# Down products one step later and a weight conversion moved from step 1 to steps 2 and 3, in a retention, ELU and gated-linear kernel

## The chip, the core and the metric

The kernel runs on one core of a Trainium2 chip. The metric is the device time of one execution in microseconds (us). The core has five engines that run their own queues in order: TensorE (matmul, PE), VectorE (DVE), ScalarE (ACT), GpSimd (POOL) and SyncE (SP, which issues most DMA transfers here). An engine waits only where an instruction needs the result, or the buffer, of another.

## The reference

All data are float32. The result must be close to this:

```python
scores = q @ k.T / sqrt(D)                      # B=4, H=8, S=576, D=64
ret    = (scores * gamma_h ** (i - j) * (i >= j)) @ v
x      = ret, heads joined                      # 2304 tokens x 512
h      = x @ w_in                               # 512 x 2048
y      = where(h > 0, h, exp(min(h, 0)) - 1) @ w_out
out    = (sigmoid(y @ w_gate) * (y @ w_val)) @ w_o2   # 1536 wide
```

## The kernel before

**Numbers.** A float32 product is made of three matmuls on a rounded part ("high") and a remainder ("low") of both operands: high x high, high x low, low x high (`mm3`). So each operand is split: ScalarE copies it to the rounded type, and another engine subtracts the copy from the original to get the remainder (`split`, L109 and L110). The weights come as raw 64-bit words and are converted on the chip in a chain of five stages (`Weight.chain`): L154 and L155 on ScalarE; L157 and L158 on VectorE; L161 (VectorE); L163 (VectorE); L169 (ScalarE copy, the high part) and L172 (remainder, on GpSimd unless the caller says `dve`). A chain works in a scratch tile `t`, whose number is the third argument of `Weight`.

**Tokens and steps.** Retention runs over 18 row tiles of 128 rows (`Step`, L226). For row tile n, `block(n)` gives TensorE `inter`(n), `scores`(n+1), `outs`(n) and `sums`(n+1), all made of 64x64 matmuls; VectorE gets `causal`(n+1) (L286), `x_mul`(n) (L347), two state additions of n+1 (L308, L312) and `x_low`(n) (L361); ScalarE `x_high`(n) (L354); GpSimd the state's decay (L313) and the scaling of v of row tile n+2 (L271).

The first pass of the feed-forward is done while retention still runs. Its steps s = 0, 1, 2, ... are `ff[s]`: 256 tokens (row tiles 2j and 2j+1, j = s//2) by one block of 128 hidden columns (f = s % 2). A step has up products (12 matmuls of 256 columns, L380), the ELU (ScalarE L393 and L394, VectorE L397), its split into high (ScalarE) and remainder (L110), and down products (12 matmuls, L114 to L116). The down products of `ff[i]` need the weights `W["o", i % 2]`, which are weights[1] and weights[3], and the tile `gt` of `ff[i]`. With f = 1 they end a sum, which ScalarE copies out of PSUM (L440).

**Order.** The program order is written out by hand and is the order of every engine's queue. In step s >= 4 the block of row tile s + 2 comes first, then up products of s; in steps 2 and 3 the up products come first and then the block. In step 1 the blocks of row tiles 2 and 3 stand behind the up products, with warm-up matmuls (`warm_up`, L122, on zeros) between. Down products of s - `LAG` (`LAG` = 2) come last in a step, from step 2 on. Each call of `stage()` gives one stage of the conversion that belongs to the step (`conv`): at its start, twice within `ups`, and once within `downs` (or, with no `downs`, at the end); the fifth stage comes at the start of the next step. weights[1] is converted in step 1 by hand, all on VectorE and ScalarE; weights[3] in step 2; weights[4] to [7] in steps 6, 9, 12 and 15; the weight `W["i", 4]` begins in step 13. The ELU tile ring `g_tile` has `LAG` + 2 = 4 tiles.

**Loads.** Row tiles from 9 on are loaded in two halves; the second half waits for the end of a feed-forward product (`begin_rest`). The load of a later weight in `loads` waits for `ff[s - LAG].end`, the last product that was issued for that step.

Of the kernel before, what the change touches and what calls it, by code (L numbers as in the profile page):

```python
# [42 lines left out]
LATE = 4  # L43
SPARE = {3: 2, 8: 2, 4: 3, 9: 3, 14: 3}
LAG = 2
FIRST_APART = 9
WARM = 12, 2, 3, 5, 4, 6

# [6 lines left out]
def retention_elu_glu(  # L55
# [13 lines left out]
    pe, act, dve, pool, sp = nc.tensor, nc.scalar, nc.vector, nc.gpsimd, nc.sync  # L69
# [11 lines left out]
    class Ring:  # L81
# [5 lines left out]
        def more(self, pool, n):  # L87
            self.homes += [(pool, f"{self.name}{len(self.homes) + i}") for i in range(n)]
# [10 lines left out]
    d_tile = Ring("d", epool, 2, [128, 256], F32)  # L99
    g_tile = Ring("g", gpool, LAG + 2, [128, 2, 512], F32R)  # L100
    t_tile = Ring("t", tpool, 2, [128, DM], I32)
# [5 lines left out]
    def split(hi, lo, src, lo_engine):  # L107

        act.copy(hi, src)  # L109
        lo_engine.tensor_tensor(out=lo, in0=src, in1=hi.bitcast(F32), op=ALU.subtract)  # L110
# [7 lines left out]
    def warm_up(n):  # L118

        h = h_bank()  # L120
        for i in range(n):
            pe.matmul(h, warm[:, :128], warm, start=True, stop=True)  # L122

    def after(ins, other):

        tc.add_manual_dep(ins.ins, other.ins.name, mybir.DependencyInfo(
            mybir.DependencyClass.Sync, mybir.DependencyReason.DATA), reason="row tiles")
        return ins
# [47 lines left out]
    def t_slot(n, f):  # L176
        if n == "i":
            return f % 2 + 3 * (f > 5 and f % 4 < 2)
        return 2 if not f % 2 or f == 2 * Q0 + 1 else 0 if f == FA - 1 else 5

    W, weights = {}, []
    for f in range(FA):
        for n, src in (("i", w_in), ("o", w_out)):
            i = len(weights)
            W[n, f] = Weight(src[f], i % 8, (0, 0, 1, 1, 0, 1, 0, 1)[i] if i < 8 else t_slot(n, f))
            weights.append(W[n, f])


# [37 lines left out]
    class Step:  # L226
# [16 lines left out]
        def load(self):  # L243
# [5 lines left out]
            if self.last:  # L249
                self.load_half(0)  # L250
            elif self.n < FIRST_APART:
                sp.dma_start(out=self.t, in_=ain[self.b, self.c].rearrange("p r x -> r p x"))
# [115 lines left out]
    class FF:  # L368
# [16 lines left out]
        def ups(self, stage, s, middle=None, end=None):  # L385
            n = self.n
            e = (d_tile if n == 256 else e_tile)()
            h = h_bank()[:, :n]
            self.up(W["i", self.f].w, h)
            if middle:  # L390
                middle()
            stage()
            act.activation(out=e, in_=h, func=AF.Relu, scale=-1.0)  # L393
            act.activation(out=e, in_=e, func=AF.Exp, scale=-1.0)  # L394
            stage()

            dve.scalar_tensor_tensor(out=e, in0=e, scalar=-1.0, in1=h, op0=ALU.add, op1=ALU.max)  # L397
            self.gt = g_tile()
            if end:
                end()  # L400
            make = lambda: split(self.gt[:, 0, :n], self.gt[:, 1, :n], e, dve if s < 2 else pool)
            if self.P and (self.f, self.g) == (3, 1):
                later.append(make)
            else:
                make()
# [396 lines left out]
    with tc.manual_schedule():  # L802
# [29 lines left out]
        dve.memset(warm, 0.0)  # L832
        early_x = g_tile(LAG + 1).bitcast(F32)
        raws = spare_y[1].bitcast(I32).rearrange("p (i c) -> p i c", i=2)
# [24 lines left out]
        def begin_rest(f):  # L859
            while rest:  # L860
                after(rest.pop(0)(), f.end)
# [24 lines left out]
        def stages(chain, n):  # L886
            for _ in range(n):
                next(chain)
# [43 lines left out]
        ff = [FF(0, j // 2, f, passes[0], j % 2 * N0, N0) for j in range(NT // N0) for f in passes[0]]  # L932
# [2 lines left out]
        end = len(ff)  # L935

        a, b = begins
        conv, loads = {2: weights[3]}, {}
        for i, w in enumerate(weights[4:8]):
            s = a + 6 + (i * (b - a - 6)) // 4  # L940
            conv[s] = w
# [79 lines left out]
        def convert(w, **engines):  # L1021

            name = name_of[id(w)]
            last = 2 if isinstance(w, Sums) else 4
            for n, _ in enumerate(w.chain(**engines)):
                if n == 3 and w not in weights[:7] and w is not W["i", 2 * Q0]:
                    more()
                if n == last and w not in weights[:8]:
                    done.append([name, 3])
                yield  # L1030
# [58 lines left out]
        for s in range(end):  # L1089
            if halves is not None:  # L1090
                next(halves, None)
            chain = halves = None
            if s in conv:
                chain = halves = made[name_of[id(conv[s])]] = convert(conv[s])
                if conv[s] is W["i", 2 * Q0 + 2]:
                    halves = None
                if conv[s] is W["i", 2 * Q0]:
                    chain = halves = islice(chain, 4)
            if s == b:
                chain = made["i", 2 * Q0]  # L1100

            def stage():
                if chain is not None:
                    next(chain, None)
                if s >= begins[1] + 4:
                    next(prepared, None)
            stage()
            if LATE <= s < NSTEP - AHEAD:
                block(s + AHEAD)
            if s == NSTEP - AHEAD:  # L1110
                more()
            middle = end_ = None
            if s == 0:
                def middle():
                    stages(w2, 1)
                    steps[2].scores()
                    steps[2].sums(True)
                    steps[2].causal()

                def end_():  # L1120
                    steps[2].states()
                    steps[3].scale()
                    steps[4].scale()
            if s == end - 1:
                def end_():
                    stage()
                    stage()
            ff[s].ups(stage if s < end - 1 else lambda: None, s, middle, end_)
            if s >= LATE:
                begin_rest(ff[s])  # L1130
            if s == 1:
                w1 = weights[1].chain(dve)
                block(2, False)
                stages(w1, 2)
                warm_up(WARM[4])
                steps[3].inter()
                steps[4].scores()
                steps[3].outs()
                steps[3].x_mul()
                steps[4].sums()  # L1140
                steps[4].causal()
                steps[3].x_high()
                steps[5].scale()
                stages(w1, 1)
                steps[3].x_low()
                steps[4].states()
                stages(w1, 2)
                for load in loads_at.get(3, []):
                    load()
                warm_up(WARM[5])  # L1150
            if 1 < s < LATE:
                block(s + AHEAD)
            if s >= LAG:
                ff[s - LAG].downs(stage)
                begin_rest(ff[s - LAG])
            else:
                stage()
            for w in loads.get(s, []):
                load = w.load()
                if s < NSTEP - AHEAD:  # L1160
                    after(load, ff[s - LAG].end)
            save()
            for i, n in enumerate(("11", "21", "22")):
                if s == begins[1] + 2 + i:
                    second.store(n)
            if s == begins[1] + 8:
                park()
                more()
            if s == begins[1] + LAG - 1:
                ret.close()  # L1170
                right = ctx.enter_context(tc.tile_pool(name="right", bufs=1, side="right"))
                e_tile.more(right, 3)
                e_tile.n = 5
                g_tile.more(right, 2)
                t_tile.more(right, 1)
                s_tile = Ring("s", right, 2, [128, 2, 2, DM], F32R)
                ps_u = ctx.enter_context(tc.tile_pool(name="ps_u", bufs=1, space=bass.MemoryType.PSUM))
                u_bank = Ring("u", ps_u, 2, [128, 512], F32)
                acc_bank = Ring("acc", None, 0, [128, 512], F32)
                acc_bank.homes = [*((ps_u, f"acc{i}") for i in (2, 3)), *((ps_acc, f"acc{i}") for i in (0, 1)), *u_bank.homes]  # L1180
                acc_bank.n = 6
# [299 lines left out]
```

## Time and profile before

| | |
|---|---|
| median of 3 runs without a profile | 871.53 us (870.1 to 873.11) |
| the profiled execution | 868.8 us |
| its span | 867.0 us |
| TensorE busy | 852.4 us, 98% of the span |
| VectorE, ScalarE, GpSimd busy | 664.7, 459.3, 409.4 us |
| mean granted clock of TensorE | 0.997 of full speed |

The span goes from the first to the last instruction of the profiled execution; its own time has 1.8 us more around it. Busy shares are means over stages with different limits. Steps 1 to 5 lie between about 22 and 57 us of the span.

### The profile page before, as it was taken

The numbers are of one execution on the slowest core, as the hardware profiler recorded it, in microseconds if no ns is written. First come the engines' busy times: TensorE is split into PE (matmuls) and PEld (weight loads), VectorE is DVE, ScalarE is ACT, GpSimd is POOL, SyncE is SP. The second block draws the span as 40 slices with busy tenths as digits, with TensorE's granted clock in tenths as the row PEclk, the third lists the DMA queues.
The fourth block names the chain that finished last, engine by engine and source line by source line (L and its number), as shares of the span: only waits on it lengthen the run. The fifth ranks groups of instructions, "written<-read, shape, count | busy, mean of one in ns | idle before, by whom it ended". The sixth has DMA issues, their size and how long they took to land.

```text
span 867.0 us, 16196 instructions
## 1 busy us (share of the span) xinstructions
PE 852.4 (98%) x6375; PEld 728.9 (84%) x6375; DVE 664.7 (77%) x967; ACT 459.3 (53%) x833; POOL 409.4 (47%) x327
## 2 busy tenths in 40 slices
PE   8899999999999999999999999999999999999998
PEld 5798998888888888888878888888888888888886
DVE  5867758789999888887887988589967564777775
ACT  3445475677666666666665665445543344343331
POOL 2445435656546543564552565244543244334453
PEclk9999999999999999999999999999999999999999
DMA  9978628745474696898774765646574665464322
GB/s 339 298 245 245 185 74 314 292 145 202 163 229 184 230 404 227 314 377 274 274 326 176 239 239 210 218 157 196 197 277 157 229 235 194 192 237 170 112 114 98
DMA packets 63852, 194.83 MB, mean 225 GB/s; under 512 B 9888, under 2 KB 19104, under 8 KB 57376
## 3 DMA queue, kind: packets, MB, share of 16 engines
q1 hardware_dynamic: 62512, 192.30, 61.8%
q10 hardware_dynamic: 1264, 1.49, 0.5%
q8 instruction: 50, 0.82, 0.4%
q14 instruction: 26, 0.21, 0.1%
HBM read 127.19 MB, written 66.58 MB: 223 GB/s over the span
## 4 chain that ended last, share of the span: by engine, by line
PE 88%; DVE 4%; DMA 3%; issue 2%; ACT 2%; POOL 1%; SPq 0%; ACTq 0%; DVEq 0%; POOLq 0%
PE u L114 13%; PE u L115 13%; PE u L116 13%; PE acc L114 10%; PE acc L115 10%; PE acc L116 10%; PE tile L114 3%; PE tile L115 3%; PE tile L116 3%; PE to L274 3%; PE h L380 2%; DMA w<-c 2%; PE h L114 1%; PE h L115 1%; PE h L116 1%
## 5 line engine op out<-in xcount | busy, mean ns | idle before, releaser
L110 POOL TENSOR_TENSOR g<-e,g 128x512 fp32r<-128x512 f32 x95 | 133.7, 1412 | 223.8 <-ACT g L109 196.8
L114 PE MATMUL u<-x,s 128*128 128x512 f32 x288 | 112.6, 391 | 0.0
L115 PE MATMUL u<-x,s 128*128 128x512 f32 x288 | 112.3, 390 | 0.0
L116 PE MATMUL u<-x,s 128*128 128x512 f32 x288 | 112.1, 389 | 0.0
L114 PE MATMUL u<-x,w 128*128 128x512 f32 (+1 forms) x264 | 98.3, 372 | 1.5 <-DMA w<-c 1.3
L115 PE MATMUL u<-x,w 128*128 128x512 f32 (+1 forms) x264 | 98.0, 371 | 0.0
L116 PE MATMUL u<-x,w 128*128 128x512 f32 (+1 forms) x264 | 97.7, 370 | 0.0
L109 ACT CAST g<-e 128x512 fp32r<-128x512 f32 x101 | 61.9, 620 | 65.0 <-DVE e L598 39.7
L172 POOL TENSOR_TENSOR w<-t,w 128x512 fp32r<-128x512 f32 x37 | 51.0, 1378 | 41.1 <-ACT w L169 37.5
L114 PEld LDWEIGHTS u<-x,s 128*128 128x128 f32 x288 | 54.1, 188 | 11.5 <-ACT u L522 0.7
L116 PEld LDWEIGHTS u<-x,s 128*128 128x128 f32 x288 | 54.1, 188 | 11.5
L115 PEld LDWEIGHTS u<-x,s 128*128 128x128 f32 x288 | 54.2, 188 | 10.3
L759 DVE TENSOR_TENSOR y<-y,tile 128x512 f32<-128x512 f32 x76 | 51.2, 680 | 10.8 <-PE tile L116 10.6
L114 PE MATMUL acc<-g,w 128*128 128x512 f32 (+1 forms) x168 | 58.2, 346 | 0.4 <-ACT y L440 0.4
L795 DVE TENSOR_TENSOR y<-y,acc 128x512 f32<-128x512 f32 x58 | 39.1, 682 | 25.4 <-PE acc L116 25.0
L114 PEld LDWEIGHTS u<-x,w 128*128 128x128 f32 x264 | 49.8, 189 | 10.2 <-DMA w<-c 1.7
L115 PE MATMUL acc<-g,w 128*128 128x512 f32 (+1 forms) x168 | 57.7, 344 | 0.0
L116 PE MATMUL acc<-g,w 128*128 128x512 f32 (+1 forms) x168 | 57.7, 343 | 0.0
L116 PEld LDWEIGHTS u<-x,w 128*128 128x128 f32 x264 | 49.7, 188 | 8.7
L115 PEld LDWEIGHTS u<-x,w 128*128 128x128 f32 x264 | 49.9, 189 | 7.4
L675 DVE TENSOR_TENSOR y<-y,acc 128x512 f32<-128x512 f32 (+1 forms) x68 | 39.6, 606 | 19.8 <-PE acc L116 17.9
L114 PE MATMUL acc<-w,g 128*128 128x512 f32 (+1 forms) x152 | 54.1, 356 | 0.0
(226 smaller groups left out, 2418.3 us busy)
## 6 DMA issues: line engine op xcount, KB each, us to landing
w<-c SPq DMA_DIRECT2D x72, 512.0 KB, 6.7
c<-w SPq DMA_DIRECT2D x48, 512.0 KB, 4.9
s<-c SPq DMA_DIRECT2D x22, 1024.0 KB, 7.1
c<-s SPq DMA_DIRECT2D x18, 1024.0 KB, 4.9
y<-y SPq DMA_DIRECT2D x8, 1024.0 KB, 6.2
in<-in_ain SPq DMA_DIRECT2D x6, 1024.0 KB, 8.9
raw<-in_w_in SPq DMA_DIRECT2D x12, 512.0 KB, 4.8
in<-in_ain SPq DMA_DIRECT2D x12, 512.0 KB, 5.3
```

The source lines that it names most:

```text
L109: act.copy(hi, src)
L110: lo_engine.tensor_tensor(out=lo, in0=src, in1=hi.bitcast(F32), op=ALU.subtract)
L114: pe.matmul(out_, wh, xh, start=start, stop=False, skip_group_check=shared)
L115: pe.matmul(out_, wh, xl, start=False, stop=False, skip_group_check=shared)
L116: return pe.matmul(out_, wl, xh, start=False, stop=stop, skip_group_check=shared)
L172: lo_engine.tensor_tensor(out=w[:, 1, :], in0=f, in1=w[:, 0, :].bitcast(F32), op=ALU.subtract)
L274: return pe.matmul(out_, w, x, start=start, stop=True, skip_group_check=True)
L380: self.end = pe.matmul(h, w[:, a, c[k]], x[:, b, k, t], start=i + k == 0, stop=i == 2 and k == KB - 1)
L675: dve.tensor_tensor(out=out_, in0=out_, in1=a, op=ALU.add)
L759: dve.tensor_tensor(out=y, in0=y, in1=a, op=ALU.add)
L795: dve.tensor_tensor(out=o, in0=o, in1=a, op=ALU.add)
```

## The change

The down products of `ff[0]` and `ff[1]` go from steps 2 and 3 to steps 3 and 4, and those of `ff[2]` and `ff[3]` both stand in step 5; from step 6 on the lag is two steps as before. The conversion of weights[1] leaves step 1, where it was written out by hand, and takes the place of weights[3] in step 2; that of weights[3] goes to step 3. weights[1] gets its remainder from GpSimd then, the default of the chain. The ELU remainders of steps 0 and 1 go from VectorE to GpSimd. The seventh weight, weights[6], uses scratch tile 1 instead of 0. The warm-up matmuls stay.

```diff
-            W[n, f] = Weight(src[f], i % 8, (0, 0, 1, 1, 0, 1, 0, 1)[i] if i < 8 else t_slot(n, f))
+            W[n, f] = Weight(src[f], i % 8, (0, 0, 1, 1, 0, 1, 1, 1)[i] if i < 8 else t_slot(n, f))
...
 LAG = 2
+DOWNS = {0: (), 1: (), 2: (), 3: (0,), 4: (1,), 5: (2, 3)}
...
-            make = lambda: split(self.gt[:, 0, :n], self.gt[:, 1, :n], e, dve if s < 2 else pool)
+            make = lambda: split(self.gt[:, 0, :n], self.gt[:, 1, :n], e, pool)
...
-        conv, loads = {2: weights[3]}, {}
+        conv, loads = {2: weights[1], 3: weights[3]}, {}
...
             if s == 1:
-                w1 = weights[1].chain(dve)
                 block(2, False)
-                stages(w1, 2)
                 warm_up(WARM[4])
                 steps[3].inter()
                 steps[4].scores()
...
                 steps[5].scale()
-                stages(w1, 1)
                 steps[3].x_low()
                 steps[4].states()
-                stages(w1, 2)
...
-            if s >= LAG:
-                ff[s - LAG].downs(stage)
-                begin_rest(ff[s - LAG])
-            else:
+            for i in DOWNS.get(s, (s - LAG,)):
+                ff[i].downs(stage)
+                begin_rest(ff[i])
+            if s < 3:
                 stage()
```

## Rows read from the trace of the kernel before

**Rows 1.** Waits of TensorE, 15 to 60 us: waiting line, releaser, total, times, longest.
```profile
PE to L274 <- DVE y L312: 1.4, 2, 0.7
```
**Rows 2.** Timeline of TensorE, 39 to 47: start, us, line, out<-in, count.
```profile
39.02 0.38 PE L114 MATMUL acc<-g,w 128*128 128x256 f32 x1
...
40.56 1.60 PE L380 MATMUL h<-x,w 128*128 128x256 f32 x12
42.09 1.08 PE L274 MATMUL to<-in,y 64*64 64x64 f32 x29
...
44.14 0.68 PE L274 MATMUL to<-in 64*64 64x64 f32 x29
...
46.38 0.27 PE L274 MATMUL to<-in,y 64*64 64x64 f32 x1
```
**Rows 3.** Timeline of VectorE, 39 to 47; in brackets idle time before and releaser.
```profile
39.13 0.69 DVE L347 TENSOR_TENSOR e<-to,cq_sb 128x512 f32<-128x512 f32 x1 [0.72 <-PE to L274]
...
41.12 1.10 DVE L163 SCALAR_TENSOR_TENSOR t<-y,t 128x512 uint32<-128x512 uint32 x1
43.64 0.42 DVE L397 SCALAR_TENSOR_TENSOR d<-d,h 128x256 f32<-128x256 f32 x1 [1.42 <-ACT d L394]
...
44.85 0.69 DVE L347 TENSOR_TENSOR e<-to,cq_sb 128x512 f32<-128x512 f32 x1 [0.19 <-PE to L274]
...
45.91 0.42 DVE L312 TENSOR_TENSOR y<-y,to 128x256 f32<-128x256 f32 x1
```
**Rows 4.** Timeline of ScalarE, 35 to 43.
```profile
35.00 0.67 ACT L154 ACTIVATE t<-y 128x512 f32<-128x512 f32 x1
...
36.13 0.38 ACT L393 ACTIVATE d<-h 128x256 f32<-128x256 f32 x1
...
42.26 0.62 ACT L169 CAST w<-t 128x512 fp32r<-128x512 f32 x1 [1.78 <-DVE t L163]
```
**Rows 5.** Timeline of VectorE, 26 to 33.
```profile
26.50 0.69 DVE L347 TENSOR_TENSOR e<-to,cq_sb 128x512 f32<-128x512 f32 x1
...
28.49 0.84 DVE L157 TENSOR_SCALAR t<-t 128x512 f32<-128x512 f32 x1
...
32.37 0.68 DVE L361 TENSOR_TENSOR x<-e,x 128x512 fp32r<-128x512 f32 x1
```
**Rows 6.** Timeline of TensorE, 25 to 33.
```profile
25.79 0.63 PE L274 MATMUL to<-y 64*64 64x64 f32 x30
...
32.03 1.47 PE L122 MATMUL h<-y 128*128 128x512 bf16 x6
```
**Rows 7.** Timeline of GpSimd, 28 to 45.
```profile
28.05 0.99 POOL L313 TENSOR_TENSOR y<-y,small 128x256 f32<-128x256 f32 x1 [1.24 <-DVE y L312]
...
41.64 1.49 POOL L271 TENSOR_TENSOR in<-in,small 128x512 f32<-128x512 f32 x1
43.10 1.27 POOL L172 TENSOR_TENSOR w<-t,w 128x512 fp32r<-128x512 f32 x1
```
**Rows 8.** Timeline of VectorE in step 13, 105 to 108.
```profile
105.12 0.43 DVE L158 TENSOR_SCALAR t<-t 128x512 uint32<-128x512 uint32 x1
...
106.53 0.68 DVE L163 SCALAR_TENSOR_TENSOR t<-raw,t 128x512 uint32<-128x512 uint32 x1
...
107.73 0.68 DVE L347 TENSOR_TENSOR e<-to,cq_sb 128x512 f32<-128x512 f32 x1
```
**Rows 9.** DMA issues on the page: count, KB each, median us to landing.
```profile
in<-in_ain SPq DMA_DIRECT2D x12, 512.0 KB, 5.3
```
**Rows 10.** Timeline of ScalarE in step 13.
```profile
102.27 0.68 ACT L154 ACTIVATE t<-raw 128x512 f32<-128x512 f32 x1 [1.40 <-POOL w L172]
```
**Rows 11.** Timeline of TensorE in step 14.
```profile
107.65 0.39 PE L114 MATMUL acc<-g,w 128*128 128x256 f32 x1 [0.41 <-ACT y L440]
```
**Rows 12.** Windows: stretch, length, busy us (instructions) by engine, TensorE's granted clock, DMA share, GB/s.
```profile
8.00:10.00 2.00, 0.47 (x18) 0.34 (x10) 1.45 (x4) 1.17 (x3) 0.29 (x1) 1.00 1.03 352
12.00:15.00 3.00, 3.00 (x68) 2.08 (x67) 2.71 (x4) 1.44 (x4) 0.87 (x1) 0.50 1.05 391
```

## The prediction

> **What bounds the kernel now.** I read the page first: TensorE is busy for nearly the whole span, so only what makes TensorE wait, or lets it start earlier, moves the time. The waits of TensorE come next, by stage. Between 15 and 60 us, where the change lives, the largest are on VectorE's last state addition (L312): 1.4 us in two waits [rows 1]. Then the timeline of each engine, to see which is late in the steps that are changed.
>
> A step is a round trip. TensorE does the up products (12 matmuls), then the retention block of a row tile: `inter`, the next `scores`, `outs`, the next `sums`. VectorE can start `x_mul` (L347) only when the last `sums` matmul is done, although it reads only what `outs` wrote: in step 2 `x_mul` begins at 39.13 after a wait on TensorE, when the products behind `sums` have already begun [rows 2, 3]. After it come the two state additions (L308, L312), and the next `inter` needs them. In step 3 `x_mul` begins at 44.85, L312 ends at 45.91 + 0.42 = 46.33, and `inter` of step 4 begins at 46.38 [rows 2, 3]. So there VectorE's chain and TensorE arrive together: the chain has no slack left. It is late because step 3 begins with the tail of a weight conversion. ScalarE's copy of the weight (L169) waits 1.78 us for VectorE's L163 and runs from 42.26; the ELU of that step queues behind it, and VectorE waits 1.42 us for the Exp before L397 at 43.64 [rows 3, 4].
>
> **The change, part by part.**
>
> *Step 1 loses the conversion of weights[1]* (three ScalarE and five VectorE instructions) and both ELU remainders leave VectorE. Does TensorE get earlier? `x_mul` of row tile 2 starts at 26.50 [rows 5]; the `sums` matmuls that it must wait for end at 25.79 + 0.63 = 26.42 [rows 6]. VectorE's queue was no more than 0.08 us later than TensorE there, so that is all that can be won; behind it, the rest of step 1 waits on that `x_mul` and on TensorE in turn. The up products of step 2 can't use an earlier `x_low` either: it starts at 32.37 [rows 5] and could start some 0.4 us sooner, but six warm-up matmuls hold TensorE from 32.03 for 1.47 us [rows 6], and those are not changed. Gain: 0 to 0.1, taken as 0.1.
>
> *Two ELU remainders go to GpSimd.* They stand in its queue behind the two scalings of row tiles 3 and 4. Their readers, down products 0 and 1, are three steps on. Cost 0; that distance is the cover. If it were gone, it would be one GpSimd operation each, near the 0.99 us of L313, which has the same width [rows 7].
>
> *Step 2 converts weights[1] instead of weights[3]*, at the same places, and has no down products. Its `x_mul` stays at 39.13, and so do L163, 41.12 to 42.22, L169, 42.26 to 42.88, and GpSimd's remainder L172, 43.10 to 44.37, since the scaling L271 from 41.64 for 1.49 stands before it [rows 3, 4, 7].
>
> *Down products 0, now in step 3.* TensorE gets to step 3 sooner by the products left out of step 2, 39.02 to 40.56 = 1.5 us. The up products start at about 39.1 and last 40.56 to 42.09 = 1.5; the block lasts from 42.09 to 44.14 + 0.68 = 2.7 [rows 2]. TensorE is through at 43.4, or at 43.8 since `sums` needs the scaling that ends at 43.13. The third matmul of the down products reads the weight's remainder, ready at 44.37. TensorE waits some 0.6 us and ends them at about 45.9.
>
> *Step 3 converts weights[3] on top.* This is the term that decides. In ScalarE's queue L154 and L155 stand between L169 (ends 42.88) and the ELU; together they take 36.13 - 35.00 = 1.13 [rows 4]. In VectorE's queue L157, L158 and L161 stand before L397, and behind L397 wait `causal`, `x_mul` and the state additions. L157 can begin at about 43.5 and meets GpSimd's L172, which runs until 44.37. A neighbour for this: L157 at 28.49 took 0.84 and ended at 29.33, 0.29 after the L313 that had begun at 28.05 and ended at 29.04 [rows 5, 7]. So L157 ends at 44.66, and L158 starts at 44.70. From L158 to L163 it is 106.53 - 105.12 = 1.41 (L158, L161, L397), and from L163 to L347 1.20 for two instructions, 0.60 each [rows 8]; with no L163 in this place, `x_mul` starts 1.41 + 0.60 = 2.01 after L158, at 46.71 instead of 44.85. That is 1.86 later, and `inter` of step 4 moves from 46.38 to 48.24. TensorE stands still from 45.9 to 48.24. The queue behind it: the scaling of row tile 7 waits on GpSimd for L313, which waits for L312; 48.24 + 0.99 + 1.49 is 50.7, and `sums` would want it at 48.24 + 2.05 = 50.3: another 0.4 [rows 2, 7].
>
> On the same collision the Trainium skill (SBUF — State Buffer, "Who interferes with whom") says that VectorE and GpSimd share a pair of ports, which one of them holds for a whole instruction while the other is blocked; an operation with two SBUF inputs takes part, and a tensor_scalar may. By that rule L157 is blocked until L172 ends, as in the sum; if it were not, L157 and L158 together would save 0.5 at most.
>
> *Down products 1, 2 and 3.* When `inter` of step 4 starts, the old kernel has done down products 1; the new one does them after it, at 1.5 us. In step 5 two sets follow each other, and from there both kernels stand at the same place.
>
> *Transfers.* The second half of row tile 9's load is released by down products 0, at 45.9 instead of 40.6. Such a load takes about 5.3 us [rows 9], so it lands at 51.2; its first reader, the scaling of row tile 9 in step 5, can't come before 48.24 + 2.7 + 1.5 + 1.5 = 53.9. Cost 0; landing later, it would hold up that scaling and its `sums` by the difference. The load of weights[4] is tied to up products already past, goes out earlier on SP's queue and into a free buffer: 0.
>
> *The other scratch tile for weights[6].* At step 13 ScalarE's L154 waits 1.40 us for GpSimd's L172, which still reads the old scratch [rows 10]. Behind it ScalarE is late with the evacuation L440, and TensorE waits 0.41 us for that [rows 11]. With another tile both waits go: a gain of 0.4.
>
> **Sum.** 1.86 + 1.5 + 0.4 - 0.4 - 0.1 = 3.3 us. The profiled execution took 868.8 (span 867.0, 1.8 around it), so it would become 872.1. The median of the runs without a profile is 871.53, 2.7 above it; there I expect 874.8. Bounds of this case: without the collision of L157 (0.5), with an undisturbed L163 (0.68 as at 106.53, not 1.10: 0.4) and no wait for the scaling (0.4) it is 2.0, 873.5; with one more VectorE operation blocked behind a whole L172 (1.27) it is 4.6, 876.1.
>
> **Rivals.**
>
> *A: the clock falls as well.* The granted clock was 0.50 from 12 to 15 us, 1.2 GHz, after a stretch (8 to 10) with only 0.47 us of TensorE work in 2.00 [rows 12]. A standstill of 2.3 us before step 4 is such a stretch. Another 3 us at half the clock lose up to 1.5 on top: 876.3. Against it: before this gap stand 1.5 us of dense down products, which the earlier stretch did not have. The skill's TensorE: Matmul & The Clock Gate ("HAM oscillation — how this bites in real kernels") also tells of waits that put the clock back to its lower level.
>
> *B: no loss that can be seen.* The delay is swallowed later, by a wait on something that comes at its own time, a transfer for instance. Then the 0.4 of step 13 is what is left: 871.1. For it: the steps that change are some 30 of 867 us. Against it: TensorE is busy nearly everywhere behind them, so there is little wait to swallow 3 us.
>
> *C: not slower, a gain in step 1.* The freed VectorE lets both waits of rows 1 vanish (1.4), and the conversion in step 3 finds room, because the ELU is not held by ScalarE; with 0.4 from step 13: 869.7. It decides from the point where `x_mul` of row tile 2 starts clearly before 26.4, and that needs `sums` earlier, which the profile doesn't give.
>
> **How the numbers follow.** Forecast 0.46, A 0.16, B 0.27, C 0.11. A difference of 0.3%, 2.6 us, is about what can be told from no change. Of the forecast's 2.0 to 4.6 some three quarters lie above it (0.34), A all (0.16): slower 0.50. B, a quarter of the forecast and half of C give 0.45 within. Faster is the rest of C, a gain beyond its price: 0.05. The range holds B at its low end and A at its high end, 870.6 to 877.2; the forecast's own is 873.5 to 876.1.
>
> **What would show it.** Right: in the new profile TensorE waits 2 us or more on VectorE's L312 before `inter` of step 4, some 9 us after the `x_mul` at about 39, and 0.3 to 0.9 us for L172 in the down products before it; `causal` (L286) of step 3 starts over 1.5 us after its `scores`; L154 of step 13 no longer waits for L172. Wrong: if `x_mul` of row tile 2 starts at 26.1 or sooner, if `inter` of step 4 starts without a wait, or if L157 in step 3 takes 0.42 beside a running L172.

## The result and the profile after

The changed kernel took 875.99 us in the median of 7 runs, the old one 870.56 us in the median of 7: a ratio of 1.0062, 95% interval 1.0045 to 1.0079, so 5.4 us (3.9 to 6.9) slower. All line numbers of the changed kernel are one higher than before, since `DOWNS` is a new line at the top.

The profiled execution took 878.24 us, span 876.5, and was the slowest of the seven, so places are compared by differences within a step, not by their times. First the waits of TensorE between 15 and 70 us: waiting line, releaser, total, times, longest. To hold against [rows 1].

```profile
PE to L275 <- DVE y L313: 3.8, 3, 2.4
PE to L275 <- issue: 1.2, 1, 1.2
...
PE to L275 <- POOL in L272: 0.4, 1, 0.4
```

The wait on the last state addition has grown from 1.4 in two waits to 3.8 in three; the third is 2.4 long. The timeline of TensorE shows where it stands:

```profile
41.97 1.70 PE L381 MATMUL h<-x,w 128*128 128x256 f32 x12
43.65 1.08 PE L275 MATMUL to<-in,y 64*64 64x64 f32 x29
...
46.18 0.69 PE L275 MATMUL to<-in 64*64 64x64 f32 x32 [0.45 <-POOL in L272]
46.80 0.39 PE L115 MATMUL acc<-g,w 128*128 128x256 f32 x1
47.03 0.28 PE L116 MATMUL acc<-g,w 128*128 128x256 f32 x1
47.42 0.39 PE L117 MATMUL acc<-g,w 128*128 128x256 f32 x1
...
51.30 0.27 PE L275 MATMUL to<-in,y 64*64 64x64 f32 x1 [2.43 <-DVE y L313]
```

Up products of step 3, block, down products 0 (the third matmul, which reads the weight's remainder, starts 0.39 after the second instead of 0.12), and then nothing for 2.43 us until `inter` of step 4. The reason is in VectorE's queue, to hold against [rows 3]:

```profile
42.12 0.69 DVE L348 TENSOR_TENSOR e<-to,cq_sb 128x512 f32<-128x512 f32 x1 [0.24 <-PE to L275]
...
44.12 1.10 DVE L164 SCALAR_TENSOR_TENSOR t<-y,t 128x512 uint32<-128x512 uint32 x1
46.48 1.18 DVE L158 TENSOR_SCALAR t<-t 128x512 f32<-128x512 f32 x1 [1.26 <-ACT t L155]
47.69 0.43 DVE L159 TENSOR_SCALAR t<-t 128x512 uint32<-128x512 uint32 x1
48.24 0.69 DVE L162 CUSTOM_DVE_ANT_0 t<-y,t 128x1024 uint16<-128x1024 uint16 x1
48.85 0.41 DVE L398 SCALAR_TENSOR_TENSOR d<-d,h 128x256 f32<-128x256 f32 x1
49.18 0.68 DVE L287 TENSOR_TENSOR a<-ts,tri 128x512 f32<-128x512 f32 x1
49.78 0.68 DVE L348 TENSOR_TENSOR e<-to,cq_sb 128x512 f32<-128x512 f32 x1
50.38 0.41 DVE L309 TENSOR_TENSOR y<-st,to 128x256 f32<-128x256 f32 x1
50.82 0.42 DVE L313 TENSOR_TENSOR y<-y,to 128x256 f32<-128x256 f32 x1
```

Between the two `x_mul` (L348) it is 49.78 - 42.12 = 7.66 us, where the old kernel had 44.85 - 39.13 = 5.72: 1.94 later, against 1.86 in the prediction. Three conversion instructions stand ahead of L398. GpSimd, to hold against [rows 7], was at the remainder of weights[1] meanwhile, and L158 ended at 47.66, 0.29 after it:

```profile
46.09 1.28 POOL L173 TENSOR_TENSOR w<-t,w 128x512 fp32r<-128x512 f32 x1
```

The windows (columns as in [rows 12]) show the granted clock behind the standstill: half of the full speed, 1.2 GHz, from about 52 to 55 (the third column from the right is the share of full speed).

```profile
50.00:52.00 2.00, 0.70 (x20) 0.70 (x22) 1.97 (x5) 0.62 (x1) 1.11 (x2) 0.94 0.13 39
52.00:54.00 2.00, 2.00 (x70) 2.00 (x68) 1.00 (x2) 0.62 (x1) 2.00 (x3) 0.50 1.02 240
54.00:56.00 2.00, 2.00 (x59) 1.93 (x54) 1.08 (x2) 0.00 (x0) 1.00 (x1) 0.71 1.13 390
```

Two more rows. At step 13 ScalarE's L155 no longer waits ([rows 10] had 1.40), and TensorE's wait for L441 ([rows 11]) is in no row. And near 91 us TensorE waited 2.09 us in the `sums` of step 10 with no releaser in the profile ("issue"), with a drop of the clock behind it; the old kernel waited 1.19 there (first line of the second fence below). The text calls this the wait near 85 us and reads it as one for TensorE's own instructions. The profile doesn't say so; what speaks for it stands under "Why the prediction was right, and where it was not".

```profile
110.48 0.67 ACT L155 ACTIVATE t<-raw 128x512 f32<-128x512 f32 x1
```
```profile
83.10 0.27 PE L274 MATMUL to<-in 64*64 64x64 f32 x1 [1.19 <-issue]
...
91.36 0.27 PE L275 MATMUL to<-in 64*64 64x64 f32 x1 [2.09 <-issue]
```
```profile
92.00:94.00 2.00, 2.00 (x14) 2.00 (x13) 1.71 (x4) 0.95 (x2) 1.00 (x2) 0.68 0.76 198
94.00:96.00 2.00, 2.00 (x11) 1.84 (x9) 0.42 (x1) 0.88 (x3) 1.67 (x3) 0.50 0.25 71
```

By the up products near 126 us (116.67 in the old kernel) the distance to the old profile is 9.7 us, and at the end of the span 9.5: the difference arises in the steps of the first pass.

### The profile page after: what moved, and what is told of

Read it like the earlier page. It is cut to its first block, busy times and chain, and to the rows that moved or that the text cites. A ratio compares the mean times of both kernels' runs of the same rounds, so it can differ in the third digit from the quotient of the medians.

```text
span 876.5 us, 16203 instructions
## 1 busy us (share of the span) xinstructions
PE 856.4 (98%) x6375; PEld 733.2 (84%) x6375; DVE 664.9 (76%) x964; ACT 459.8 (52%) x833; POOL 412.1 (47%) x330
## 4 chain that ended last, share of the span: by engine, by line
PE 89%; DVE 3%; DMA 3%; issue 2%; ACT 1%; POOL 1%; SPq 0%; DVEq 0%; POOLq 0%; ACTq 0%
PE u L115 13%; PE u L116 13%; PE u L117 13%; PE acc L117 10%; PE acc L116 10%; PE acc L115 10%; PE to L275 4%; PE tile L115 3%; PE tile L116 3%; PE tile L117 3%; PE h L381 3%; DMA w<-c 2%; PE ts L275 1%; PE h L115 1%; PE h L116 1%
```

## The experiments

Theory V: the conversion in step 3 holds VectorE's chain, and the standstill lets the clock fall. Theory L: the later down products and what lies elsewhere cost the time, not the conversion. Ratios are to the old kernel on the same chip, with 95% intervals. The last section of this part holds all lengths of steps in one table.

**conversion_back.** The changed kernel with both conversions in their old places.

```diff
-        conv, loads = {2: weights[1], 3: weights[3]}, {}
+        conv, loads = {2: weights[3]}, {}
...
             if s == 1:
+                w1 = weights[1].chain(dve)
                 block(2, False)
+                stages(w1, 2)
...
+                stages(w1, 1)
                 steps[3].x_low()
                 steps[4].states()
+                stages(w1, 2)
```

> The changed kernel with the two conversions where they were (weights[1] in step 1, weights[3] in step 2); later down products, scratch tile and ELU remainders as changed. Theory V (weights[3]'s conversion in step 3 holds VectorE's chain, and the gap that it opens lets the clock fall): inter of step 4 waits for VectorE under 1 us instead of 2.4, no drop of the granted clock behind it, and the time is some 1.3 us above the old kernel (1.5 for the down products that no longer cover the round trip, 0.4 less for the scratch tile), near 872. Theory L (the later down products and waits ahead of step 2 cost it, not the conversion): the wait is gone or not, but the time stays 4 us or more above the old kernel, near 875.

Measured: 874.73 us, ratio 1.0032 (1.0016 to 1.0049). The wait before `inter` of step 4 is gone (0.4 in the second profile of this kernel): in its list of waits (10 to 100 us) there are only the two of step 1 left on L313, and `x_mul` comes 44.86 - 39.34 = 5.52 after the one before it.

```profile
PE to L275 <- issue: 3.7, 5, 2.0
PE to L275 <- DVE y L313: 1.4, 2, 0.7
```

So V is right on the place, but not on the size: 2.8 us are left instead of 1.3. One wait without a releaser near 85 us is 2.0 long, where the old kernel had 1.2; with the clock that fell behind it, steps 9 and 10 are 2.7 longer in this profile.

**conversion_behind_block.** The same work in the same step, but the stages come behind the block.

```diff
+            held_back = [s == 3]
+
             def stage():
-                if chain is not None:
+                if chain is not None and not held_back[0]:
                     next(chain, None)
...
             if 1 < s < LATE:
                 block(s + AHEAD)
+            if held_back[0]:
+                held_back[0] = False
+                for _ in range(3):
+                    stage()
```

> The changed kernel, with one difference: in step 3 the stages of weights[3]'s conversion stand behind the retention block instead of ahead of it, so that causal, x_mul and the state additions pass them in VectorE's queue, and the ELU passes L154 and L155 in ScalarE's. Theory V: inter of step 4 waits under 1 us, no clock drop there, near 872 (1 to 2 us above the old kernel), though the same work is done in the same step. Theory L: near 876, as the changed kernel.

Measured: 875.44, ratio 1.0041 (1.0024 to 1.0058). The order alone takes the 2.4 us wait away (0.23 before that `inter`), as V expects, but the weight is then late for down products 1, which wait 0.9 for its remainder and 0.2 for the high part. Steps 3 to 5 are 1.8 shorter than in the changed kernel, and the ratio is 1.8 us lower (1.0041 against 1.0062), which agrees; the two intervals overlap, so the time alone does not show it.

```profile
PE acc L117 <- POOL w L173: 0.9, 1, 0.9
```

**gap_filled.** Ten warm-up matmuls where TensorE stood still.

```diff
             for i in DOWNS.get(s, (s - LAG,)):
                 ff[i].downs(stage)
                 begin_rest(ff[i])
+            if s == 3:
+                warm_up(10)
```

> The changed kernel with ten warm-up matmuls (on zeros, 2.1 us at the full clock) between the down products of step 3 and the block of step 4, where TensorE stood still for 2.4 us. If the standstill there lets the granted clock fall (rival A of the prediction, part of theory V): no drop from 52 to 55 us, and the time is 1 to 1.5 us below the changed kernel, near 874.7. If the clock falls for another reason, or its fall there costs nothing: the time stays near 876.

Measured: 873.44, ratio 1.0019 (1.0001 to 1.0038), 3.7 us less than the changed kernel by the ratios, where 1 to 1.5 were expected. More work on TensorE made the kernel faster. The clock is not lowered behind the gap:

```profile
50.00:52.00 2.00, 1.85 (x105) 1.65 (x101) 1.03 (x2) 0.62 (x1) 2.00 (x2) 1.00 0.91 218
52.00:54.00 2.00, 2.00 (x17) 2.00 (x18) 1.90 (x4) 0.90 (x2) 0.80 (x2) 1.00 1.08 412
```

But the wait near 85 us is also down to 0.6, which a filled gap does not explain. Hence the next run.

**instructions_shifted.** Ten matmuls of 64 columns in that place.

```diff
+            if s == 3:
+                h = h_bank()
+                for i in range(10):
+                    pe.matmul(h[:, :64], warm[:, :128], warm[:, :64], start=True, stop=True)
```

> The changed kernel with ten tiny matmuls (64 columns on zeros, some 0.3 us in all) at the place where the run gap_filled had ten long ones (2.1 us). TensorE's later instructions fall differently into the blocks in which its code is loaded, as there, but the gap of 2.4 us is not filled. If gap_filled won because the standstill no longer lets the clock fall, this run stays near the changed kernel, 875 to 876.5, with a clock drop behind the gap. If it won because the code is loaded at other moments, this run wins the same and comes to 873.5 or below 874.

Measured: 873.77, ratio 1.0038 (1.0024 to 1.0052). Neither expectation alone: the gap stays (the wait on L313 is 2.1 there), no clock drop follows it in this profile, and the wait near 85 us is 1.5 without a drop.

```profile
48.73 0.27 PE L275 MATMUL to<-in,y 64*64 64x64 f32 x1 [2.12 <-DVE y L313]
```
```profile
50.00:52.00 2.00, 1.55 (x87) 1.35 (x80) 0.99 (x2) 0.62 (x1) 2.00 (x2) 1.00 1.05 234
```

By the ratios more than half of what gap_filled won against the changed kernel comes without the filling; but the interval of this run overlaps with that of the changed kernel and with that of gap_filled, so neither part can be told from nothing by the time. A standstill of over 2 us lowered the clock in the profiles of the changed kernel and of remainder_on_vector, and not in this one; so rival A holds for some executions and not for all.

**remainder_on_vector.** The remainder of weights[1] on VectorE.

```diff
-                chain = halves = made[name_of[id(conv[s])]] = convert(conv[s])
+                chain = halves = made[name_of[id(conv[s])]] = convert(conv[s], **({"lo_engine": dve} if s == 2 else {}))
```

> The changed kernel with the remainder (L173, old L172) of weights[1] on VectorE instead of GpSimd, so that nothing on GpSimd runs beside L157 and L158 of step 3 (lines 158 and 159 in the changed kernel). By the prediction's term for the collision: that L157 takes about 0.42 us instead of 1.18, the remainder is ready some 0.7 us sooner, x_mul and inter of step 4 come about 0.5 us sooner, the standstill shrinks from 2.4 to near 2 (by the earlier end of the down products a little less), and the time falls by about 0.5, to 875.5; if the shorter standstill saves the clock too, to 874. If the collision is not what makes that L157 long: 1.18 stays and so does the time.

Measured: 874.52, ratio 1.0040 (1.0024 to 1.0056), which is not told apart from the changed kernel by time. The profile settles the term: with no GpSimd operation beside it L158 takes 0.41, and `x_mul` comes 46.57 - 39.56 = 7.01 after the one before it, 0.65 sooner. The standstill before `inter` of step 4 is 2.15 instead of 2.43, since the down products end sooner too. The rule of the Trainium skill that the prediction weighed (SBUF — State Buffer, "Who interferes with whom") agrees with these rows: by it L158 is blocked until the GpSimd operation ends, and it took 1.18 us beside one and 0.41 without.

```profile
43.34 0.77 DVE L173 TENSOR_TENSOR w<-t,w 128x512 fp32r<-128x512 f32 x1 [0.69 <-ACT w L170]
44.03 0.41 DVE L158 TENSOR_SCALAR t<-t 128x512 f32<-128x512 f32 x1
```

**Second profiles.** The same kernels once more, no edit.

> The kernel of the run conversion_back once more, for a second profile. In its first one TensorE lost 2.0 us at one place near 85 us with nothing to wait for but its own instructions, and the clock fell behind it. If that belongs to the kernel: 1.7 us or more at the same place again, and the time again above 873.5. If it is chance: another length (the old kernel showed 1.2 there), and a time that follows it.

> The old kernel once more, for a second profile. Its first one had a wait for instructions of 0.9 us in step 2 and of 1.2 near 82 us, and one drop of the clock (12 to 15 us). If these are chance, their lengths and places differ here by some tenths to a few us while the waits on VectorE (0.6 to 0.9 us each in step 1) stay the same to 0.1.

One run each: 875.67 and 871.83. The wait near 85 us is 2.8 in the one and 1.1 in the other (first profiles 2.0 and 1.2), as expected if it belongs to the kernel; two profiles of each make that likely, not certain. In step 1, however, the second profile of the old kernel, which has no part of the change, shows a drop of the clock (0.50 from 32 to 38 us), as the changed kernel's profile does; so that loss can't be put down to the change.

```profile
PE to L275 <- issue: 2.8, 1, 2.8
```
```profile
PE to L274 <- issue: 1.1, 1, 1.1
```

**small_parts_alone.** The old kernel with scratch tile 1 for weights[6] and both ELU remainders on GpSimd.

```diff
-            W[n, f] = Weight(src[f], i % 8, (0, 0, 1, 1, 0, 1, 0, 1)[i] if i < 8 else t_slot(n, f))
+            W[n, f] = Weight(src[f], i % 8, (0, 0, 1, 1, 0, 1, 1, 1)[i] if i < 8 else t_slot(n, f))
...
-            make = lambda: split(self.gt[:, 0, :n], self.gt[:, 1, :n], e, dve if s < 2 else pool)
+            make = lambda: split(self.gt[:, 0, :n], self.gt[:, 1, :n], e, pool)
```

> The old kernel with only the two small parts of the change: scratch tile 1 for weights[6], and the ELU remainders of steps 0 and 1 on GpSimd. By the prediction: L154 of step 13 no longer waits 1.40 us for L172, the wait of TensorE for the evacuation (0.41) is gone, and the time is 0.4 us lower, near 870.2, within the noise. Rival: the two GpSimd operations hold up VectorE or the state decay, and the time is 1 us or more higher.

Measured: 870.69, ratio 0.9992 (0.9973 to 1.0011): no difference that can be told, as expected. The two remainders run on GpSimd behind the two scalings, and L154 of step 13 follows L169 at once:

```profile
24.64 2.06 POOL L271 TENSOR_TENSOR y<-y,small 128x512 f32<-128x512 f32 x2
26.66 1.42 POOL L110 TENSOR_TENSOR g<-d,g 128x256 fp32r<-128x256 f32 x2
...
102.50 0.66 ACT L154 ACTIVATE t<-raw 128x512 f32<-128x512 f32 x1
```

**conversion_back_shifted and small_parts_shifted.** The ten tiny matmuls of instructions_shifted at the end of step 3 in these two kernels.

> The kernel of the run conversion_back (down products later, both conversions where they were) with the ten tiny matmuls (0.3 us) at the end of step 3. Both profiles of conversion_back lost 2.0 and 2.8 us near 85 us waiting for instructions, with a drop of the clock behind it, where the old kernel lost 1.1 to 1.2 and had no drop. Theory: that place is part of what the later down products cost (some 2 to 2.5 of the 2.8 to 3.2 us), because the code is loaded at another moment against the transfers; shifted, the wait there is 1.5 or less, no drop follows, and the time is 1 to 2 us lower, near 873 (ratio 1.001 to 1.002). Rival: the whole loss lies in steps 2 to 5, and the time stays at 1.003 or above.

> The kernel of the run small_parts_alone (down products at their old places) with the same ten tiny matmuls at the end of step 3: the control for the shift. If a shift helps only where the later down products had made the wait near 85 us long: here it changes nothing or costs its 0.3 us, and the ratio is 0.999 to 1.001. If a shift of the code is worth 1 to 2 us to any version: 0.998 or less, and then this version beats both kernels.

Measured: 872.12, ratio 1.0006 (0.9991 to 1.0021), down from 1.0032; and 870.20, ratio 0.9981 (0.9965 to 0.9997), against 0.9992 without the shift. By the ratios the shift is worth over 2 us where the down products are later, and 1 us or nothing where they are not. The wait near 85 us is gone in both, the 1.2 us of the old kernel too. In conversion_back_shifted the only wait without a releaser between 80 and 95 us is this, in the down products near 80 us:

```profile
PE acc L116 <- issue: 0.3, 1, 0.3
```

small_parts_shifted has the lowest ratio here, by an interval that barely leaves 1 out.

These two kernels differ in nothing but the place of the down products, and ran on the same chip: 872.12 - 870.20 = 1.9 us (0.8 to 2.7, a 95% interval from drawing the 12 runs of each again). That is the price of the later down products where the wait near 85 us is out of the way. The same pair without the shift is conversion_back and small_parts_alone: 874.73 - 870.69 = 4.0 us (1.3 to 5.7). By the profiles the two differences part in steps 9 and 10, which are 0.7 longer in the shifted pair and 2.7 in the other (table below).

Why a shift helps is not wholly shown: gap_filled and the shifted runs also take one of the two `h` banks once more, so that the up products behind them use the other one. No run tries that alone.

**Lengths of steps.** Worked out from the starts of the up products in the timelines of TensorE, in us. Steps 3 to 5 contain down products 1, 2 and 3 in the old kernel and in small_parts, and 0 to 3 in the others; the extra set is 1.5. The last column is the wait "issue" between 80 and 95 us. Step 9 to step 11 is the length of steps 9 and 10.

| kernel | step 3 to step 6 | step 9 to step 11 | wait |
|---|---|---|---|
| old kernel, first and second profile | 19.15, 19.18 | 12.53, 12.40 | 1.2, 1.1 |
| small_parts_alone | 19.93 | 12.56 | 1.2 |
| small_parts_shifted | 19.04 | 11.36 | none |
| conversion_back, two profiles | 22.62, 22.89 | 15.21, 16.92 | 2.0, 2.8 |
| conversion_back_shifted | 22.73 | 12.07 | 0.3 |
| conversion_behind_block | 23.61 | 14.75 | 1.9 |
| changed kernel | 25.41 | 14.89 | 2.1 |
| remainder_on_vector | 24.82 | 13.65 | 2.2 |
| instructions_shifted | 24.61 | 13.23 | 1.5 |
| gap_filled | 24.49 | 12.05 | 0.6 |

## Why the prediction was right, and where it was not

The direction and the place were right, the size was not. The median lies above the forecast (874.8), near rival A's 876.3 and within the forecast's own bounds (873.5 to 876.1); but those were put on 871.53, the old kernel's median of 3 runs, and its median of 7 is 870.56. As a difference the 5.4 us lie above the forecast's 3.3, above its upper bound of 4.6 and above rival A's 4.8. That the time itself lies so near is in part luck with the base.

- *Step 1 gains nothing.* Right. `x_mul` of row tile 2 still waits for TensorE, 0.24 us, though VectorE's queue is empty before it; removing the conversion removed no wait.
- *The conversion in step 3, 1.86.* Right. 1.94 between the two `x_mul`; by lengths of steps, 24.6 and 24.5 (no clock drop) against 22.6 to 22.9 with the conversion back: 1.6 to 2.0. Of this 0.65 is the collision of L158 with GpSimd (L158 itself is 0.77 shorter without it), which was put at 0.5.
- *Down products 1 done later, 1.5, and 0.4 for the scaling.* Steps 3 to 5 of conversion_back are 3.4 to 3.7 longer than before, 1.9 to 2.2 without the set that moved in, and the pair of shifted kernels measures 1.9: right in sum, 1.9 predicted. The parts are less sure: the wait of `sums` in step 4 for the scaling (0.4) stands in the profile of instructions_shifted (0.45), not in that of the changed kernel, where the clock was low; and in conversion_back there are 0.4 and 0.3 us of waits without a releaser in its place. The wait of down products 0 for the weight's remainder was 0.3 instead of 0.6, because two of their matmuls come before the one that waits.
- *The scratch tile, -0.4.* The waits went, as said. The time of small_parts_alone agrees with it and with nothing.
- *"From there both kernels stand at the same place."* This step failed. The wait without a releaser in step 10 is 1.9 to 2.8 in five profiles with later down products, against 1.1 to 1.2 in three without; with the shift it is 0.6 and 1.5 in two kernels with later down products and gone in conversion_back_shifted and small_parts_shifted. With the drop of the clock that followed it in four of the five, steps 9 and 10 were 2.2 to 4.5 longer (1.1 in the fifth). No term of the sum had it. Shown is that it goes with the later down products and shrinks or goes with a shift. That it is a wait for instructions is argued from times: in all ten profiles that have it, it ended 1.1 to 1.5 us after a packet of the instruction queue had landed, however long it was. Why that packet comes later there is open.
- *Rival A* came true in part: the clock fell behind the standstill in the changed kernel's profile, 25.41 against 24.6, so 0.8 us; of the three kernels that left the gap open it fell in two.

Sum by the table: 1.9 (conversion) + 2.0 (down products) + 0.8 (clock) + 2.4 (steps 9 and 10) - 0.4 = 6.7 for executions in which the clock falls at both places. The clock does not fall in every one, and the median lost 5.4. The only run of the changed kernel with a mean granted clock of 1.00 took 873.62, which is 2.8 above 870.8, the median of the old kernel's 15 runs (of 35 in the first set of experiments) with 0.999 or more. That is near the 3.3 of the forecast, but it is one run, from another set than those 15, and conversion_back's only run with 1.00 took 873.27, 0.35 less, where the conversion's term is 1.9: single runs don't settle the sum.

## What to carry to other kernels

Ask of work that is moved later what it covered where it stood: these down products filled TensorE's time while VectorE finished its round trip, and without them the same round trip is a wait. Before a conversion is put into a step, look at which queue is the last to finish there; VectorE was busy for 77% of the span, but in that step its chain ended only 0.05 us before TensorE needed it. And a change of 1 to 5 us in a kernel of many small matmuls should be tried with its instructions shifted by a few, old and new alike: here the later down products cost 4.0 us without the shift and 1.9 with it.

## What the runs showed of the hardware

- Ten tiny matmuls, put some 35 to 40 us before the place, made a wait of 2.0 and 2.8 us without a releaser go away, and took the ratio from 1.0032 to 1.0006; in the kernel with the down products at their old places a wait of 1.2 us went as well.
- The clock of TensorE fell behind such waits: of eight waits of 1.9 to 2.8 us (before step 4 and near 85 us) six were followed by 3 to 7 us at 1.2 GHz; after 1.5 or less near 85 us the clock did not fall. Behind a standstill of 2.1 us before step 4 (instructions_shifted) and one of 2.2 near 85 us (remainder_on_vector) it stayed at 2.4 GHz.
- A tensor_scalar on VectorE that started during a GpSimd operation took 1.18 us and ended 0.29 after it; with none beside it, in the same place, it took 0.41.
